# Folding an output gate into the output weights, and moving a bias product one chunk earlier, in a DiT attention block

## The chip, the cores and the metric

The kernel runs on one core of one Trainium2 chip. The metric is the device time of one execution in microseconds (us). The engines are called PE (matmul), Vector or DVE, Scalar or ACT, GpSimd or POOL, and SP, whose queue issues the loads and stores. The kernel's tiles lie in SBUF, but for those that PE writes its results to, which lie in PSUM. A run counts as slow when it is over 1.5% above the fastest run of the same kernel, otherwise as fast. Medians are of all runs of a kernel, ratios of its fast runs alone.

## The reference, cut to what matters

```python
B, N, D = 2, 256, 1152          # all bf16
mod = (silu(c) @ w_mod).reshape(B, 6, 1, D)
shift_a, scale_a, gate_a = mod[:, 0], mod[:, 1], mod[:, 2]
h = layernorm(x) * (1 + scale_a) + shift_a
q, k, v = split(h @ wqkv)
p = softmax(q @ k.T * D ** -0.5)
out = x + gate_a * ((p @ v) @ wo)
```

`gate_a` has one value per batch and output column. Multiplying the result by it is therefore the same as multiplying the columns of `wo` by it, once per batch.

## The kernel before: the parts that matter

There are four row tiles of 128 tokens, two per batch, and nine chunks of 128 along D. k is computed from the scaled rows alone, `hTk`, because a shift of k changes all scores of a row by the same amount, which the softmax removes. q and v need `hT = hTk + shift`. The shift comes out of 81 small matmuls (`m_shift`), which stand between the k chunks. In program order, the last 36 of them follow the last k chunk:

```python
k_chunks([0, 1])                     # per chunk: 9 matmuls 128x128 by 128x512, one cast to SBUF
for j in range(2, KC):
    k_chunks([j])
    if j == 6: m_shift.do(range(0, 5))
    if j == 8:
        m_shift.do(range(5, KC))
        make_hT()                    # copies shiftT out of PSUM, then 18 adds of 128x256,
                                     # dealt out to Vector, GpSimd, Scalar in turn
q_chunks([0, 1])
for j in range(2, KC): q_chunks([j])
```

The gate is computed and broadcast over the partitions between the v tiles (81 small matmuls, then 18 broadcasts by matmul, cast to `gate_bc`). The output stage applies it with two Vector operations per tile:

```python
for tt in range(TT):
    for (f0, fw) in FB:              # (0, 512), (512, 512), (1024, 128)
        ... ps = sum over dk of oT[:, dk, tt] x wo_sb[:, dk, f0:f0+fw] ...
        nc.vector.scalar_tensor_tensor(out=tmp, in0=ps, scalar=rinv[:, tt:tt+1],
                                       in1=gate_bc[:, b, f0:f0+fw], op0=mult, op1=mult)
        nc.vector.tensor_tensor(out=y, in0=tmp, in1=x_sb[:, tt, f0:f0+fw], op=add)
        nc.sync.dma_start(out=out_flat[...], in_=y)
```

PE's results for q, k, v and y rotate through three PSUM tiles (pool `ps_acc`). Vector and Scalar share the casts that empty the q, k and v ones; Vector empties those of y.

## Time and profile before

| | before |
|---|---|
| time, median of the first 4 runs | 107.05 us (106.48 to 108.79) |
| span in the profile | 104.7 us |
| PE busy | 97.3 us, 93% |
| Vector busy | 43.9 us, 42% |

The page's first part gives each engine's busy time, share of the span and instruction count. Its second cuts the span into 40 slices of 2.6 us; a digit is the busy share in tenths. PEld is the loading of weights for PE, PEclk the share of its clock that PE was granted.

```profile
PE 97.3 (93%) x786; PEld 54.0 (52%) x786; DVE 43.9 (42%) x100; ACT 25.2 (24%) x60; POOL 6.3 (6%) x14
...
PE   5996998999999699999999999999999999999940
...
DVE  1696229302202342220221552232257847678780
...
PEclk9999999999999999999999999999999999999999
```

PE is full from the eighth slice on, except for one dip (the 6 in slice 14, about 36 us) and the end. Vector is idle more than half of the time. So only three things can shorten this kernel with the same matmuls: the first 16 us, the dip, and the tail.

The dip in the timeline of the kernel before. Columns: start and length in us, engine, source line, operation, outputs and inputs, count; in brackets the idle time of the engine before it and who ended it.

```profile
34.62 1.04 PE L75 MATMUL ps_shift<-scT,wm_sh 128*128 128x2 bf16 x36
...
35.70 0.18 DVE L313 COPY shiftT<-ps_shift 128x18 f32<-128x18 f32 x1 [2.13 <-PE ps_shift L75]
35.91 1.77 DVE L322 TENSOR_SCALAR hT<-hTk,shiftT 128x256 bf16<-128x256 bf16 x6
35.98 2.50 ACT L327 ACTIVATE hT<-hTk,shiftT 128x256 bf16<-128x256 bf16 x6 [0.57 <-DVE shiftT L313]
...
36.60 1.67 PE L75 MATMUL ps_q<-hT,wq_sb 128*128 128x512 bf16 x7 [0.93 <-POOL hT L324]
```

The shift products end, the shift is copied out, the first two pieces of `hT` are made, and only then can q start: PE is idle 0.93 us.

The tail in the timeline of the kernel before:

```profile
82.97 17.71 PE L75 MATMUL ps_y<-wo_sb,oT 128*128 128x512 bf16 x108
...
99.06 0.69 DVE L462 TENSOR_TENSOR y<-tmp,x_sb 128x512 bf16<-128x512 f32 x1
100.22 1.01 DVE L457 SCALAR_TENSOR_TENSOR tmp<-ps_y,rinv,gate_bc 128x512 f32<-128x512 f32 x2 [0.47 <-PE ps_y L75]
101.14 0.89 DVE L462 TENSOR_TENSOR y<-tmp,x_sb 128x512 bf16<-128x512 f32 x2
```

After the last matmul Vector still runs one pass over the last two tiles (512 and 128 wide), then a second one. Before that, Vector waited for PE at the y tiles, as the waits view says (who waited for whom; total us, times, longest):

```profile
DVE tmp L457 <- PE ps_y L75: 5.3, 8, 1.5
...
PE ps_q L75 <- POOL hT L324: 0.9, 1, 0.9
```

No line of that view has PE waiting for Vector in the y stage. The two operations per y tile cost time only at the very end.

### The profile page before, as it was taken

The numbers are of one execution on the slowest core, as the hardware profiler recorded it, in microseconds if no ns is written. First come the engines' busy times: TensorE is split into PE (matmuls) and PEld (weight loads), VectorE is DVE, ScalarE is ACT, GpSimd is POOL, SyncE is SP. The second block draws the span as 40 slices with busy tenths as digits, with TensorE's granted clock in tenths as the row PEclk, the third lists the DMA queues.
The fourth block names the chain that finished last, engine by engine and source line by source line (L and its number), as shares of the span: only waits on it lengthen the run. The fifth ranks groups of instructions, "written<-read, shape, count | busy, mean of one in ns | idle before, by whom it ended". The sixth has DMA issues, their size and how long they took to land.

```text
span 104.7 us, 1898 instructions
## 1 busy us (share of the span) xinstructions
PE 97.3 (93%) x786; PEld 54.0 (52%) x786; DVE 43.9 (42%) x100; ACT 25.2 (24%) x60; POOL 6.3 (6%) x14
## 2 busy tenths in 40 slices
PE   5996998999999699999999999999999999999940
PEld 2325774444464544444447846664599745555420
DVE  1696229302202342220221552232257847678780
ACT  4079017220120472022022541110246500000000
POOL 2044000000000280000000000000000000000000
PEclk9999999999999999999999999999999999999999
DMA  2999957999999999999999900000000001222212
GB/s 68 351 370 367 387 132 193 312 329 384 392 370 330 326 332 356 387 390 390 394 391 358 254 12 6 0 0 0 6 0 3 0 0 50 69 87 76 65 51 63
DMA packets 19332, 21.07 MB, mean 201 GB/s; under 512 B 2811, under 2 KB 14203, under 8 KB 19323
## 3 DMA queue, kind: packets, MB, share of 16 engines
q1 hardware_dynamic: 19323, 20.95, 60.6%
q8 instruction: 6, 0.10, 0.4%
q14 instruction: 3, 0.02, 0.1%
HBM read 19.76 MB, written 1.18 MB: 200 GB/s over the span
## 4 chain that ended last, share of the span: by engine, by line
PE 61%; issue 26%; DVE 6%; DMA 3%; POOL 1%; POOLq 1%; DVEq 0%
PE ps_q L75 17%; PE ps_v L75 17%; PE ps_y L75 16%; PE ps_o L75 4%; PE ps_s L75 4%; DVE stats L171 3%; DMA x_sb<-in_x_dram 3%; PE ps_gate L75 2%; POOL xn L225 1%; PE ps_g L75 1%; DVE tmp L457 1%; DVE y L462 1%; POOLq L489 1%; DVE mv L175 0%; PE ps_p L78 0%
## 5 line engine op out<-in xcount | busy, mean ns | idle before, releaser
L75 PE MATMUL ps_v<-wv_sb,hT 128*128 128x512 bf16 (+1 forms) x108 | 19.2, 325 | 0.0
L75 PE MATMUL ps_q<-hT,wq_sb 128*128 128x512 bf16 x81 | 17.6, 379 | 0.9 <-POOL hT L324 0.9
L75 PE MATMUL ps_k<-hTk,wk_sb 128*128 128x512 bf16 x81 | 17.8, 379 | 0.3 <-DVE hTk L296 0.3
L75 PE MATMUL ps_y<-wo_sb,oT 128*128 128x512 bf16 (+1 forms) x108 | 17.7, 326 | 0.0
L75 PEld LDWEIGHTS <-oT 128*128 128x128 bf16 x108 | 9.2, 98 | 8.5
L75 PEld LDWEIGHTS <-wq_sb 128*128 128x128 bf16 x81 | 7.9, 98 | 10.2 <-issue 0.9
L75 PEld LDWEIGHTS <-wk_sb 128*128 128x128 bf16 x81 | 7.7, 98 | 9.9 <-issue 0.8
L75 PEld LDWEIGHTS <-hT 128*128 128x128 bf16 x108 | 8.9, 98 | 7.1
L457 DVE SCALAR_TENSOR_TENSOR tmp<-ps_y,rinv,gate_bc 128x512 f32<-128x512 f32 (+1 forms) x12 | 7.0, 615 | 5.3 <-PE ps_y L75 5.3
L141 DVE CAST qT<-ps_q 128x512 bf16<-128x512 f32 x5 | 3.5, 692 | 13.8 <-PE ps_q L75 13.8
L141 DVE CAST kT<-ps_k 128x512 bf16<-128x512 f32 x4 | 2.8, 692 | 12.3 <-PE ps_k L75 12.3
L141 DVE CAST v_sb<-ps_v 128x512 bf16<-128x512 f32 x5 | 3.5, 691 | 7.7 <-PE ps_v L75 7.2
L139 ACT CAST kT<-ps_k 128x512 bf16<-128x512 f32 x5 | 2.9, 586 | 14.9 <-PE ps_k L75 14.9
L462 DVE TENSOR_TENSOR y<-tmp,x_sb 128x512 bf16<-128x512 f32 (+1 forms) x12 | 6.3, 553 | 0.1
L75 PE MATMUL ps_w<-zeros 128*128 128x512 bf16 x10 | 4.4, 632 | 1.2 <-DVE zeros L124 1.2
L171 DVE BATCH_NORM_STATS2 stats<-x_sb 128x6 f32<-128x384 bf16 x9 | 4.5, 537 | 2.4 <-DMA x_sb<-in_x_dram 2.4
L139 ACT CAST v_sb<-ps_v 128x128 bf16<-128x128 f32 (+1 forms) x7 | 2.8, 403 | 10.5 <-PE ps_v L75 10.3
L139 ACT CAST qT<-ps_q 128x512 bf16<-128x512 f32 x4 | 2.3, 586 | 12.1 <-PE ps_q L75 12.1
L141 DVE CAST gate_bc<-ps_g 128x512 bf16<-128x512 f32 (+1 forms) x6 | 3.2, 555 | 3.4 <-PE ps_g L75 3.3
L324 POOL TENSOR_SCALAR hT<-hTk,shiftT 128x256 bf16<-128x256 bf16 x6 | 3.0, 515 | 26.0 <-DVE shiftT L313 26.0
L75 PEld LDWEIGHTS <-wm_sc 128*128 128x128 bf16 x94 | 3.3, 96 | 2.0 <-issue 1.3
L75 PE MATMUL ps_s<-kT,qT 128*128 128x256 bf16 x36 | 4.1, 272 | 0.0
(62 smaller groups left out, 78.5 us busy)
## 6 DMA issues: line engine op xcount, KB each, us to landing
wm_sc<-in_w_mod_dram SPq DMA_DIRECT2D x9, 288.0 KB, 5.3
wm_sh<-in_w_mod_dram SPq DMA_DIRECT2D x9, 288.0 KB, 6.4
wq_sb<-in_wqkv_dram SPq DMA_DIRECT2D x3, 864.0 KB, 10.5
wm_g<-in_w_mod_dram SPq DMA_DIRECT2D x9, 288.0 KB, 7.4
wo_sb<-in_wo_dram SPq DMA_DIRECT2D x9, 288.0 KB, 6.0
wv_sb<-in_wqkv_dram SPq DMA_DIRECT2D x2, 1152.0 KB, 9.7
x_sb<-in_x_dram SPq DMA_DIRECT2D x4, 288.0 KB, 3.5
wk_sb<-in_wqkv_dram SPq DMA_DIRECT2D x2, 576.0 KB, 5.5
```

Of the source, the lines that this page charges most:

```text
L75: return _pin(nc.tensor.matmul(*a, **kw))
L139: nc.scalar.copy(out=out_ap, in_=in_ap)
L141: nc.vector.tensor_copy(out=out_ap, in_=in_ap)
L171: pin("dve", nc.vector.bn_stats(out=stats_t[tt][:, s, :], in_=x_sb[:, tt, s * SUBW:(s + 1) * SUBW]))
L225: nc.gpsimd.tensor_scalar(out=xn[:, tt, :], in0=x_sb[:, tt, :], scalar1=rstd[:, 0:1], scalar2=nmr[:, 0:1], op0=ALU.mult, op1=ALU.add,)
L324: nc.gpsimd.tensor_scalar(out=o_ap, in0=i_ap, scalar1=1.0, scalar2=shiftT[:, k, b:b + 1], op0=ALU.mult, op1=ALU.add)
L457: nc.vector.scalar_tensor_tensor(out=tmp[:, :fw], in0=ps[:, :fw], scalar=rinv[:, tt:tt + 1], in1=gate_bc[:, b, f0:f0 + fw], op0=ALU.mult, ...
L462: nc.vector.tensor_tensor(out=y[:, :fw], in0=tmp[:, :fw], in1=x_sb[:, tt, f0:f0 + fw], op=ALU.add)
L489: with _tile.TileContext(nc) as tc:
```

## The change

The intent: scale `wo` by the gate beforehand, once per batch (the fold: 18 multiplications of 128x1152, nine per batch), while Vector has time, so that the epilogue is one operation; compute the gate early enough for that; and make `hT` behind the last k chunk instead of after it.

```diff
-    load_cols(wv_sb, Wv, 0, 512)
     wm_g = wmpool.tile(...); load_rows(wm_g, w_mod[:, 2 * D:3 * D], range(KC))
+    load_cols(wv_sb, Wv, 0, 512)
...
-                # hT adds on Vector, GpSimd and Scalar in turn
+                nc.vector.tensor_scalar_add(hT[...], hTk[...], shiftT[:, k, b:b + 1])
...
-        if j == 6:
+        if j == 5:
             m_shift.do(range(0, 5))
-        if j == 8:
+        if j == 7:
             m_shift.do(range(5, KC))
             make_hT()
... # m_gate.do and gate_bcast move from between the v tiles to between the q chunks
+    wo_g = [wpool.tile([P, KC, D], BF16, name="wo_g0", tag="wk"),    # in the place of wk and wq
+            wpool.tile([P, KC, D], BF16, name="wo_g1", tag="wq")]
+    def fold_gate(b, dk, eng):
+        e = nc.vector if eng == "dve" else nc.gpsimd
+        e.tensor_tensor(out=wo_g[b][:, dk, :], in0=wo_sb[:, dk, :], in1=gate_bc[:, b, :], op=ALU.mult)
... # 9 folds after p_transposes(1, 0), 9 after v_tile(1, 2), all on Vector
-                mm(..., rhs=wo_sb[:, dk, f0:f0 + fw], ...)
-            tmp = ps * rinv * gate_bc        # scalar_tensor_tensor
-            y = tmp + x_sb                   # tensor_tensor
+                mm(..., rhs=wo_g[b][:, dk, f0:f0 + fw], ...)
+            y = ps * rinv + x_sb             # scalar_tensor_tensor
```

The rest of the diff renames helpers. The compiler's scheduler spreads the 18 folds among the score maxima and the casts of v in Vector's order.

More of the change, by code (lines that the diff above doesn't have):

```diff
@@ L56 @@
     _nosync = mybir.DependencyInfo(mybir.DependencyClass.NoSync, mybir.DependencyReason.DATA)
-    _pe_prev = [None]
-    def _pin(inst):
-        if _pe_prev[0] is not None:
-            tc.add_manual_dep(inst.ins, _pe_prev[0].ins.name, _nosync, reason="pe order")
-        _pe_prev[0] = inst
-        return inst
     _chains = {}
@@ L74, in mm @@
     def mm(*a, **kw):
-        return _pin(nc.tensor.matmul(*a, **kw))
+        return pin("pe", nc.tensor.matmul(*a, **kw))
     def tr(*a, **kw):
-        return _pin(nc.tensor.transpose(*a, **kw))
+        return pin("pe", nc.tensor.transpose(*a, **kw))
     x_sb = act.tile([P, TT, D], BF16, name="x_sb")
@@ L97 @@
     wm_sh = wmpool.tile([P, KC, D], BF16, name="wm_sh", tag="wm")
-    wk_sb = wpool.tile([P, KC, D], BF16, name="wk_sb")
-    wq_sb = wpool.tile([P, KC, D], BF16, name="wq_sb")
+    wk_sb = wpool.tile([P, KC, D], BF16, name="wk_sb", tag="wk")
+    wq_sb = wpool.tile([P, KC, D], BF16, name="wq_sb", tag="wq")
     wv_sb = wpool.tile([P, KC, D], BF16, name="wv_sb")
@@ L153, in do @@
                 for j in range(KC):
-                    mm(
-                        self.ps[:, j, :], lhsT=self.wm[:, k, j * P:(j + 1) * P], rhs=scT[:, k, :],
-                        start=self.first, stop=(k == KC - 1 and j == KC - 1), skip_group_check=True,
-                    )
+                    mm(self.ps[:, j, :], lhsT=self.wm[:, k, j * P:(j + 1) * P], rhs=scT[:, k, :],
+                       start=self.first, stop=(k == KC - 1 and j == KC - 1), skip_group_check=True)
                     self.first = False
@@ L162 @@
     SUBW = D // NSUB
+    stats_t = {}
     mvs = {}
-    stats_t = {}
     def ln_bnstats(tt, subs):
@@ L175, in ln_aggr, with ln_rstd, ln_act_mean @@
         pin("dve", nc.vector.bn_aggr(out=mv[:], in_=stats_t[tt][:]))
-        mvs[tt] = (mv, None, None)
-    def ln_rstd(tt):
-        mv = mvs[tt][0]
+        mvs[tt] = [mv[:, 0:1], mv[:, 1:2], None, None]
+    def ln_rstd(tt, var_scale=1.0):
         lnv = small.tile([P, 1], FP32, name="lnv")
-        pin("act", nc.scalar.activation(out=lnv[:], in_=mv[:, 1:2], func=ACT.Ln, bias=eps_t[:, 0:1], scale=1.0))
+        pin("act", nc.scalar.activation(out=lnv[:], in_=mvs[tt][1], func=ACT.Ln, bias=eps_t[:, 0:1],
+                                        scale=var_scale))
         rstd = small.tile([P, 1], FP32, name="rstd")
         pin("act", nc.scalar.activation(out=rstd[:], in_=lnv[:], func=ACT.Exp, scale=-0.5))
-        mvs[tt] = (mv, rstd, None)
+        mvs[tt][2] = rstd[:, 0:1]
     def ln_nmr(tt):
-        mv, rstd, _ = mvs[tt]
         nmr = small.tile([P, 1], FP32, name="nmr")
-        pin("dve", nc.vector.scalar_tensor_tensor(out=nmr[:], in0=mv[:, 0:1], scalar=-1.0, in1=rstd[:],
+        pin("dve", nc.vector.scalar_tensor_tensor(out=nmr[:], in0=mvs[tt][0], scalar=-1.0, in1=mvs[tt][2],
                                                   op0=ALU.mult, op1=ALU.mult))
-        mvs[tt] = (mv, rstd, nmr)
-    def ln_stats_UNUSED(tt, need_nmr):
-        mv = None
-        rstd = None
-        mvs[tt] = (mv, rstd, None)
-    def ln_stats_act_mean(tt):
+        mvs[tt][3] = nmr[:, 0:1]
+    def ln_act_mean(tt):
         mean = small.tile([P, 1], FP32, name="mean_a")
@@ L203, in ln_stats_act_mean, with ln_act_var @@
         pin("act", nc.scalar.activation(out=negmean[:], in_=mean[:], func=ACT.Copy, scale=-1.0))
-        mvs[tt] = (mean, negmean)
-    def ln_stats_act_var(tt):
-        mean, negmean = mvs[tt]
+        mvs[tt] = [mean[:, 0:1], None, None, negmean[:, 0:1]]
+    def ln_act_var(tt):
         ssq = small.tile([P, 1], FP32, name="ssq_a")
-        pin("act", nc.scalar.activation(out=xn[:, tt, :], in_=x_sb[:, tt, :], func=ACT.Square, bias=negmean[:, 0:1],
-                                        scale=1.0, accum_out=ssq[:, 0:1]))
-        lnv = small.tile([P, 1], FP32, name="lnv")
-        pin("act", nc.scalar.activation(out=lnv[:], in_=ssq[:], func=ACT.Ln, bias=eps_t[:, 0:1], scale=1.0 / D))
-        rstd = small.tile([P, 1], FP32, name="rstd")
-        pin("act", nc.scalar.activation(out=rstd[:], in_=lnv[:], func=ACT.Exp, scale=-0.5))
-        mvs[tt] = (mean, rstd, None)
+        pin("act", nc.scalar.activation(out=xn[:, tt, :], in_=x_sb[:, tt, :], func=ACT.Square,
+                                        bias=mvs[tt][3], scale=1.0, accum_out=ssq[:, 0:1]))
+        mvs[tt][1] = ssq[:, 0:1]
+        ln_rstd(tt, var_scale=1.0 / D)
     def ln_norm(tt, eng):
-        mv, rstd, nmr = mvs[tt]
+        mean, _, rstd, nmr = mvs[tt]
         if eng == "dve":
-            pin("dve", nc.vector.tensor_scalar(
-                out=xn[:, tt, :], in0=x_sb[:, tt, :], scalar1=mv[:, 0:1], scalar2=rstd[:, 0:1],
-                op0=ALU.subtract, op1=ALU.mult,
-            ))
-        else:
-            nc.gpsimd.tensor_scalar(
-                out=xn[:, tt, :], in0=x_sb[:, tt, :], scalar1=rstd[:, 0:1], scalar2=nmr[:, 0:1],
-                op0=ALU.mult, op1=ALU.add,
-            )
+            pin("dve", nc.vector.tensor_scalar(out=xn[:, tt, :], in0=x_sb[:, tt, :], scalar1=mean, scalar2=rstd,
+                                               op0=ALU.subtract, op1=ALU.mult))
+        else:
+            nc.gpsimd.tensor_scalar(out=xn[:, tt, :], in0=x_sb[:, tt, :], scalar1=rstd, scalar2=nmr,
+                                    op0=ALU.mult, op1=ALU.add)
     ptiles = [ps_tr.tile([P, 2, TT, P], BF16, name=f"ps_xT{g}", tag="tr") for g in range(4)]
@@ L242 @@
     ln_rstd(0)
-    ln_stats_act_mean(3)
+    ln_act_mean(3)
     ln_bnstats(1, range(2)); ln_nmr(0); ln_bnstats(1, [2]); ln_aggr(1)
@@ L251 @@
     ln_rstd(1)
-    ln_stats_act_var(3)
+    ln_act_var(3)
     ln_bnstats(2, range(2))
@@ L255 @@
     pin("dve", nc.vector.reciprocal(out=e_t[:], in_=e_t[:]))
-    pin("dve", nc.vector.tensor_tensor(
-        out=scT[:].rearrange("p k b -> p b k"),
-        in0=ps_c[:].rearrange("p (b k) -> p b k", b=B),
-        in1=e_t[:].rearrange("p (b k) -> p b k", b=B),
-        op=ALU.mult,
-    ))
+    pin("dve", nc.vector.tensor_tensor(out=scT[:].rearrange("p k b -> p b k"),
+                                       in0=ps_c[:].rearrange("p (b k) -> p b k", b=B),
+                                       in1=e_t[:].rearrange("p (b k) -> p b k", b=B), op=ALU.mult))
     ln_nmr(1); ln_bnstats(2, [2]); ln_aggr(2)
@@ L287 @@
     ACT_CHUNKS = (1, 4, 6)
-    mcnt = 0
     for k in range(KC):
@@ L301, with proj_chunks @@
     shiftT = const.tile([P, KC, B], FP32, name="shiftT")
-    def k_chunks(js):
-        pss = [ps_acc.tile([P, T], FP32, name="ps_k", tag="acc") for _ in js]
+    def proj_chunks(w_sb, src, dst, js, nm):
+        pss = [ps_acc.tile([P, T], FP32, name=nm, tag="acc") for _ in js]
         for k in range(KC):
             for ji, j in enumerate(js):
-                mm(pss[ji][:], lhsT=wk_sb[:, k, j * P:(j + 1) * P], rhs=hTk[:, k, :],
-                                 start=(k == 0), stop=(k == KC - 1))
+                mm(pss[ji][:], lhsT=w_sb[:, k, j * P:(j + 1) * P], rhs=src[:, k, :],
+                   start=(k == 0), stop=(k == KC - 1))
         for ji, j in enumerate(js):
-            evac(kT[:, j, :], pss[ji][:])
+            evac(dst[:, j, :], pss[ji][:])
     def make_hT():
         nc.vector.tensor_copy(out=shiftT[:], in_=m_shift.ps[:])
-        engs = ["dve", "pool", "act"]
-        cnt = 0
         for k in range(KC):
             for b in range(B):
-                o_ap = hT[:, k, b * N:(b + 1) * N]
-                i_ap = hTk[:, k, b * N:(b + 1) * N]
-                e = engs[cnt % 3]
-                if e == "dve":
-                    nc.vector.tensor_scalar_add(o_ap, i_ap, shiftT[:, k, b:b + 1])
-                elif e == "pool":
-                    nc.gpsimd.tensor_scalar(out=o_ap, in0=i_ap, scalar1=1.0,
-                                            scalar2=shiftT[:, k, b:b + 1], op0=ALU.mult, op1=ALU.add)
-                else:
-                    nc.scalar.activation(out=o_ap, in_=i_ap, func=ACT.Identity,
-                                         scale=1.0, bias=shiftT[:, k, b:b + 1])
-                cnt += 1
-    k_chunks([0, 1])
+                nc.vector.tensor_scalar_add(hT[:, k, b * N:(b + 1) * N], hTk[:, k, b * N:(b + 1) * N],
+                                            shiftT[:, k, b:b + 1])
+    proj_chunks(wk_sb, hTk, kT, [0, 1], "ps_k")
     for j in range(2, KC):
-        k_chunks([j])
-        if j == 6:
+        proj_chunks(wk_sb, hTk, kT, [j], "ps_k")
+        if j == 5:
             m_shift.do(range(0, 5))
-        if j == 8:
+        if j == 7:
             m_shift.do(range(5, KC))
@@ L340, with gate_bcast @@
     qT = act.tile([P, KC, T], BF16, name="qT", tag="C")
-    def q_chunks(js):
-        pss = [ps_acc.tile([P, T], FP32, name="ps_q", tag="acc") for _ in js]
-        for k in range(KC):
-            for ji, j in enumerate(js):
-                mm(pss[ji][:], lhsT=wq_sb[:, k, j * P:(j + 1) * P], rhs=hT[:, k, :],
-                   start=(k == 0), stop=(k == KC - 1))
-        for ji, j in enumerate(js):
-            evac(qT[:, j, :], pss[ji][:])
-    q_chunks([0, 1])
-    for j in range(2, KC):
-        q_chunks([j])
+    gateT = const.tile([P, KC, B], BF16, name="gateT")
+    gate_bc = act.tile([P, B, D], BF16, name="gate_bc")
+    m_gate = ModT(wm_g, "gate")
+    def gate_bcast(b, j0):
+        jn = min(4, KC - j0)
+        ps_g = ps_tr.tile([P, T], FP32, name="ps_g", tag="tr")
+        for jj in range(jn):
+            j = j0 + jj
+            mm(ps_g[:, jj * P:(jj + 1) * P], lhsT=gateT[:, j, b:b + 1].to_broadcast([P, P]),
+               rhs=ident[:], start=True, stop=True)
+        evac(gate_bc[:, b, j0 * P:(j0 + jn) * P], ps_g[:, :jn * P])
+    proj_chunks(wq_sb, hT, qT, [0, 1], "ps_q")
+    for j in range(2, KC):
+        proj_chunks(wq_sb, hT, qT, [j], "ps_q")
+        if j == 4:
+            m_gate.do(range(0, 3))
+        if j == 5:
+            m_gate.do(range(3, 6))
+        if j == 6:
+            m_gate.do(range(6, 9))
+            nc.vector.tensor_copy(out=gateT[:], in_=m_gate.ps[:])
+        if j == 7:
+            gate_bcast(0, 0)
+            gate_bcast(0, 4)
+        if j == 8:
+            gate_bcast(0, 8)
+            gate_bcast(1, 0)
+    wo_g = [wpool.tile([P, KC, D], BF16, name="wo_g0", tag="wk"),
[3 more added lines that the diff above has]
+        e.tensor_tensor(out=wo_g[b][:, dk, :], in0=wo_sb[:, dk, :], in1=gate_bc[:, b, :], op=ALU.mult)
     FB = [(0, 512), (512, 512), (1024, 128)]
@@ L360 @@
     pT = act.tile([P, B, QT, N], BF16, name="pT")
-    gateT = const.tile([P, KC, B], BF16, name="gateT")
-    gate_bc = act.tile([P, B, D], BF16, name="gate_bc")
-    m_gate = ModT(wm_g, "gate")
     def v_tile(fi, tt):
@@ L368, in v_tile @@
         for k in range(KC):
-            mm(ps[:, :fw], lhsT=hT[:, k, tt * P:(tt + 1) * P],
-                             rhs=wv_sb[:, k, f0:f0 + fw],
-                             start=(k == 0), stop=(k == KC - 1))
+            mm(ps[:, :fw], lhsT=hT[:, k, tt * P:(tt + 1) * P], rhs=wv_sb[:, k, f0:f0 + fw],
+               start=(k == 0), stop=(k == KC - 1))
         evac(v_sb[:, tt, f0:f0 + fw], ps[:, :fw])
@@ L377, in scores @@
         for dk in range(KC):
-            mm(ps_s[:, :N], lhsT=qT[:, dk, tq * P:(tq + 1) * P],
-                             rhs=kT[:, dk, b * N:(b + 1) * N],
-                             start=(dk == 0), stop=(dk == KC - 1))
+            mm(ps_s[:, :N], lhsT=qT[:, dk, tq * P:(tq + 1) * P], rhs=kT[:, dk, b * N:(b + 1) * N],
+               start=(dk == 0), stop=(dk == KC - 1))
         mx = small.tile([P, 1], FP32, name="mx")
@@ L393, in p_transposes @@
         evac(pT[:, b, :, qi * P:(qi + 1) * P], ps_p[:, 0, :QT, :])
-    def gate_bcast(b, j0):
-        jn = min(4, KC - j0)
-        ps_g = ps_tr.tile([P, T], FP32, name="ps_g", tag="tr")
-        for jj in range(jn):
-            j = j0 + jj
-            mm(ps_g[:, jj * P:(jj + 1) * P], lhsT=gateT[:, j, b:b + 1].to_broadcast([P, P]),
-                             rhs=ident[:], start=True, stop=True)
-        evac(gate_bc[:, b, j0 * P:(j0 + jn) * P], ps_g[:, :jn * P])
     v_tile(0, 0)
+    gate_bcast(1, 4)
+    gate_bcast(1, 8)
     scores(0, 0)
@@ L413 @@
     p_transposes(0, 1)
-    m_gate.do(range(0, 3))
     v_tile(0, 3)
     p_transposes(1, 0)
-    m_gate.do(range(3, 6))
+    for dk in range(KC):
+        fold_gate(0, dk, "dve")
     v_tile(1, 0)
     p_transposes(1, 1)
-    m_gate.do(range(6, 9))
-    nc.vector.tensor_copy(out=gateT[:], in_=m_gate.ps[:])
     v_tile(1, 1)
     v_tile(1, 2)
-    gate_bcast(0, 0)
+    for dk in range(KC):
+        fold_gate(1, dk, "dve")
     v_tile(1, 3)
-    gate_bcast(0, 4)
     v_tile(2, 0)
-    gate_bcast(0, 8)
     v_tile(2, 1)
-    gate_bcast(1, 0)
     v_tile(2, 2)
-    gate_bcast(1, 4)
     v_tile(2, 3)
-    gate_bcast(1, 8)
     oT = act.tile([P, KC, T], BF16, name="oT", tag="B")
@@ L444 @@
                     mm(ps_o[:, dd * N:(dd + 1) * N], lhsT=v_sb[:, b * QT + kt, dk * P:(dk + 1) * P],
-                                     rhs=pT[:, b, kt, :], start=(kt == 0), stop=(kt == QT - 1))
+                       rhs=pT[:, b, kt, :], start=(kt == 0), stop=(kt == QT - 1))
             evac(oT[:, dk0:dk0 + dn, b * N:(b + 1) * N], ps_o[:, :dn * N].rearrange("p (a n) -> p a n", a=dn))
@@ L452 @@
             for dk in range(KC):
-                mm(ps[:, :fw], lhsT=oT[:, dk, tt * P:(tt + 1) * P],
-                                 rhs=wo_sb[:, dk, f0:f0 + fw],
-                                 start=(dk == 0), stop=(dk == KC - 1))
-            tmp = work.tile([P, 512], FP32, name="tmp")
-            nc.vector.scalar_tensor_tensor(
-                out=tmp[:, :fw], in0=ps[:, :fw], scalar=rinv[:, tt:tt + 1],
-                in1=gate_bc[:, b, f0:f0 + fw], op0=ALU.mult, op1=ALU.mult,
-            )
+                mm(ps[:, :fw], lhsT=oT[:, dk, tt * P:(tt + 1) * P], rhs=wo_g[b][:, dk, f0:f0 + fw],
+                   start=(dk == 0), stop=(dk == KC - 1))
             y = work.tile([P, 512], BF16, name="y")
-            nc.vector.tensor_tensor(out=y[:, :fw], in0=tmp[:, :fw], in1=x_sb[:, tt, f0:f0 + fw], op=ALU.add)
+            nc.vector.scalar_tensor_tensor(out=y[:, :fw], in0=ps[:, :fw], scalar=rinv[:, tt:tt + 1],
+                                           in1=x_sb[:, tt, f0:f0 + fw], op0=ALU.mult, op1=ALU.add)
             nc.sync.dma_start(out=out_flat[tt * P:(tt + 1) * P, f0:f0 + fw], in_=y[:, :fw])
```

## The prediction

> **What bounds it now.** The tensor engine. In the page's busy table PE is busy 97.3 of 104.7 us (93%); by stretch it is busy 100% from 36.6 to 100.2 us (q, v, scores, output), at full clock. Vector is busy 42%. The matmuls stay 786, so only PE's gaps and the two ends can be gained.
>
> The gaps the change can touch:
> 1. Before q. The waits view shows PE idle 0.93 us before the first ps_q, ended by the GpSimd hT add: the shift product ends at 35.66, then come the shiftT copy and hT adds, and ps_q starts at 36.60. The 81 ps_q then take 17.64 us where the v-tile pace (1.94 us per 9) gives 17.44: 0.2 us lost to hT pieces.
> 2. The tail. The last 128x512 ps_y is done at 100.2. Then tmp 512 (751 ns), tmp 128 (343), y 512 (687), y 128 (286); the last store is issued at 102.28 and lands at 103.8.
>
> **What the change does.**
> - Shift products are one k chunk earlier, so shiftT and hT overlap chunk 8 (1.94 us). hT goes to Vector alone: 18 adds. In the trace Vector's hT add beside GpSimd takes 364 ns (295 from start to start); I estimate 0.21-0.28 us alone, which keeps up with q's 0.43 us per two pieces. The first wq third landed at 34.92, before q would start at 35.66. Saving 0.9-1.1 us.
> - tmp+y become one op, PSUM input, about 0.75 us as tmp. At the tail the last store goes out at about 101.4: saving 0.85 us. Other y tiles gain nothing: Vector waited for PE.
> - Gate products and broadcasts move from v into q. Same PE work: zero. wm_g is loaded before the first wv part, so it lands about 3 us earlier (by 47), wanted from 45.4 to 50: in time.
> - New: 18 folds wo*gate, 128x1152 bf16 on Vector, scheduled between the score maxima and the v casts. [...] No op of this kind is in the trace.
>
> **Where folds could cost.** The ps_v tiles rotate over three buffers, PE makes one in about 2.05 us. On the scheduled order Vector does two folds and one 692 ns cast per ps_v: 2.1-2.2 us. I reckon the first Vector v cast about 2.5-3 us late, later ones 3.3-4 us late, where about 3.4 is free. So PE stalls 0 to 0.6 us in v; I take 0.25. Folds end near 77, before y starts (82).
>
> **Sum.** -1.0 (q start) -0.85 (tail) +0.25 = -1.6 us of 107.05: 105.4 us, range 104.6 to 106.5. Chances: faster by over 2% 0.25, within 2% 0.69, slower 0.06.
>
> **What would show it.** (a) the wait ps_q <- hT is gone and ps_q directly follows ps_k; (b) one Vector op after the last ps_y, last store issued about 0.85 us sooner after the last ps_y than before; (c) fold mean 0.70-0.80 us; (d) PE waits on v casts under 0.6 us in total; (e) no wait of ps_y for wo_g, and no wait for wm_g or wv.
>
> **What would make it wrong.** [...] 24 us of Vector work would stall v by 4 us or more, making it slower. hT adds alone as slow as 0.36 us from start to start: q stalls over 1 us in its first pair. A late wm_g or wo row would hold PE or Vector. No stall at all and hT perfect: -2 us, close to the 2% line.

The sum came to -1.6 us: -1.0 for the start of q, -0.85 for the tail, +0.25 for stalls of PE in v. The trace after has 750 ns for a fold, by which two folds and a cast of 692 ns add up to 2.19 us. What 24 us of folds do is measured in e8 (18 times 1345 ns). The 0.21-0.28 us of an hT add was an estimate; the trace before has 273 to 509 ns, with GpSimd and Scalar adding as well.

## The result

| | before | after |
|---|---|---|
| median | 106.98 us (16 runs, 106.48 to 108.79) | 104.98 us (11 runs, 104.50 to 105.66) |
| span in the profile | 104.7 us | 102.9 us |

The ratio is 0.9823, with a 95% interval of 0.9799 to 0.9847. The gain of 1.8% is clear of noise, and lies across the 2% line with its interval.

The page of the kernel after, the same parts:

```profile
PE 97.0 (94%) x786; PEld 53.8 (52%) x786; DVE 50.6 (49%) x118; ACT 22.4 (22%) x54; POOL 3.3 (3%) x8
...
PE   5996998999999999999999999999999999999970
...
DVE  1596309312011962220224999999924844233450
```

The dip is gone. Vector has more work than before, a solid row of nines from slice 23 to 29, and lower digits in the last ten slices.

Timeline of the kernel after, at the start of q:

```profile
32.86 1.04 PE L67 MATMUL ps_shift<-scT,wm_sh 128*128 128x2 bf16 x36
...
33.77 2.10 PE L67 MATMUL ps_k<-hTk,wk_sb 128*128 128x512 bf16 x9
33.94 0.18 DVE L284 COPY shiftT<-ps_shift 128x18 f32<-128x18 f32 x1 [0.19 <-PE ps_shift L67]
34.15 3.03 DVE L287 TENSOR_SCALAR hT<-hTk,shiftT 128x256 bf16<-128x256 bf16 x15
...
35.70 1.67 PE L67 MATMUL ps_q<-hT,wq_sb 128*128 128x512 bf16 x7
```

The copy and the adds run while PE does the last k chunk; `ps_q` starts with no bracket, that is with no idle time before it. The tail, and one stretch of the v stage, in the timeline of the kernel after:

```profile
67.32 0.68 DVE L133 CAST v_sb<-ps_v 128x512 bf16<-128x512 f32 x1
67.92 1.42 DVE L335 TENSOR_TENSOR wo_g<-wo_sb,gate_bc 128x1152 bf16<-128x1152 bf16 x2
...
68.14 0.28 PE L70 MATMUL ps_p<-ident,p_all 128*128 128x128 bf16 x2
...
69.25 0.68 DVE L133 CAST v_sb<-ps_v 128x512 bf16<-128x512 f32 x1
...
82.08 17.71 PE L67 MATMUL ps_y<-wo_g,oT 128*128 128x512 bf16 x108
...
99.33 1.01 DVE L420 SCALAR_TENSOR_TENSOR y<-ps_y,rinv,x_sb 128x512 bf16<-128x512 f32 x2 [1.19 <-PE ps_y L67]
```

At the tail one Vector pass is left. In the v stage Vector alternates between a cast and two folds. The v tile that ended when `ps_p` began (68.14, its last results about 0.2 us later) was cast from 69.25 on, about 0.9 us late.

The time from the first instruction to the first `ps_k` differs from run to run (16.0 to 18.6 us among the profiles with the same head), with the arrival of the first loads and, in the slowest of them (e9's), a lower clock there: its mean over the span is 0.984, with 1.00 in every window from 16 to 94 us and `ps_y` at its usual pace up to 103.5 us. Spans of single profiles are therefore poor to compare. The stretches between the first starts of PE's groups repeat to 0.02 us in kernels with the same code in them, and the table is worked out from those starts:

| stretch, us | before | after | difference |
|---|---|---|---|
| first ps_k to first ps_q | 20.58 | 19.51 | -1.07 |
| first ps_q to first ps_v | 17.48 | 20.24 | +2.76 |
| first ps_v to first ps_o | 24.96 | 22.21 | -2.75 |
| first ps_o to first ps_y | 3.93 | 3.93 | 0.00 |
| first to last ps_y | 17.49 | 17.49 | 0.00 |
| last ps_y to the end | 4.21 | 3.36 | -0.85 |

The gate's matmuls moved from v to q and cost the same there (2.76 against 2.75 us). What is left is 1.07 us at the start of q and 0.85 us at the tail, 1.92 us in all, beside 2.0 us between the medians.

### The profile page after: what moved, and what is told of

It reads as the page before. It is cut to its first block, busy times and chain, and to the rows that moved or that the text cites. A ratio compares the mean times of both kernels' runs of the same rounds, so it can differ in the third digit from the quotient of the medians.

```text
span 102.9 us, 1906 instructions
## 1 busy us (share of the span) xinstructions
PE 97.0 (94%) x786; PEld 53.8 (52%) x786; DVE 50.6 (49%) x118; ACT 22.4 (22%) x54; POOL 3.3 (3%) x8
## 4 chain that ended last, share of the span: by engine, by line
PE 81%; DMA 12%; SPq 2%; issue 1%; DVEq 0%; DVE 0%
PE ps_k L67 17%; PE ps_v L67 17%; PE ps_q L67 17%; PE ps_y L67 17%; DMA wm_sc<-in_w_mod_dram 6%; DMA x_sb<-in_x_dram 4%; PE ps_o L67 4%; PE ps_s L67 4%; DMA wk_sb<-in_wqkv_dram 2%; PE ps_shift L67 2%; PE ps_gate L67 2%; SPq L74 1%; PE ps_g L67 1%; SPq L80 1%; DVEq L448 0%
## 5 line engine op out<-in xcount | busy, mean ns | idle before, releaser
L67 PE MATMUL ps_v<-wv_sb,hT 128*128 128x512 bf16 (+1 forms) x108 | 18.3, 326 | 0.0
L67 PE MATMUL ps_q<-hT,wq_sb 128*128 128x512 bf16 x81 | 18.3, 379 | 0.0
L67 PE MATMUL ps_y<-wo_g,oT 128*128 128x512 bf16 (+1 forms) x108 | 17.7, 326 | 0.0
L335 DVE TENSOR_TENSOR wo_g<-wo_sb,gate_bc 128x1152 bf16<-128x1152 bf16 x18 | 13.0, 750 | 0.0
L420 DVE SCALAR_TENSOR_TENSOR y<-ps_y,rinv,x_sb 128x512 bf16<-128x512 f32 (+1 forms) x12 | 7.0, 614 | 10.6 <-PE ps_y L67 10.6
L133 DVE CAST v_sb<-ps_v 128x512 bf16<-128x512 f32 (+1 forms) x8 | 4.7, 586 | 2.9 <-PE ps_v L67 2.9
L67 PE MATMUL ps_scale<-scT,wm_sc 128*128 128x2 bf16 x81 | 3.3, 163 | 1.0 <-DVE nmr L177 1.0
L67 PE MATMUL ps_o<-pT,v_sb 128*128 128x256 bf16 x36 | 4.1, 273 | 0.0
L67 PE MATMUL ps_w<-wm_sc 128*128 128x512 bf16 x13 | 4.1, 376 | 0.0
```

The lines of the kernel that those rows point to most:

```text
L67: return pin("pe", nc.tensor.matmul(*a, **kw))
L133: nc.vector.tensor_copy(out=out_ap, in_=in_ap)
L335: e.tensor_tensor(out=wo_g[b][:, dk, :], in0=wo_sb[:, dk, :], in1=gate_bc[:, b, :], op=ALU.mult)
L420: nc.vector.scalar_tensor_tensor(out=y[:, :fw], in0=ps[:, :fw], scalar=rinv[:, tt:tt + 1], in1=x_sb[:, tt, f0:f0 + fw], op0=ALU.mult, op1= ...
```

## The experiments

Theory A: the gain is the sum of two independent parts. The head start of one k chunk takes away the gap before q, and the short epilogue pays at the last tile alone. Rivals: that freeing Vector from GpSimd closes the gap (B); that the shorter epilogue pays all along the output stage (C). A further question is why the folds cost nothing, where I had expected up to 0.6 us. All runs gave correct results.

| run | ratio to before | 95% interval | ps_k to ps_q | ps_v to ps_y | last ps_y to end |
|---|---|---|---|---|---|
| before | | | 20.58 | 28.89 | 4.21 |
| after | 0.9823 | 0.9799 to 0.9847 | 19.51 | 26.14 | 3.36 |
| e1_shift_and_dve | 0.9899 | 0.9872 to 0.9927 | 19.51 | 28.89 | 4.22 |
| e2_shift_only | 0.9894 | 0.9870 to 0.9918 | 19.60 | 28.89 | 4.21 |
| e3_dve_only | 0.9992 | 0.9964 to 1.0020 | 20.52 | 28.89 | 4.21 |
| e4_fold_only | 0.9935 | 0.9909 to 0.9962 | 20.60 | 26.35 | 3.37 |
| e5_no_fold | 0.9918 | 0.9854 to 0.9982 | 19.51 | 26.14 | 4.21 |
| e6_fold_b1 | 0.9833 | 0.9786 to 0.9880 | 19.51 | 26.14 | 3.36 |
| e7_three_more | 0.9823 | 0.9788 to 0.9857 | 19.50 | 26.14 | 3.36 |
| e9_nine_more | 0.9958 | 0.9899 to 1.0016 | 19.51 | 27.68 | 3.36 |
| e8_fold_fp32 | 1.0537 | 1.0464 to 1.0611 | 19.50 | 34.14 | 3.36 |

The last three columns are us between first starts, as above; from ps_v to ps_y, kernels with the gate in q have 2.75 us less than those with it in v. In e4 the records of two ps_y matmuls are missing, probably the first among them, so its 26.35 is too long by one matmul (the stretch behind it is shorter by the same 0.22).

### The two parts of the change alone

e1_shift_and_dve, from the kernel before:

```diff
-        if j == 6:
+        if j == 5:
             m_shift.do(range(0, 5))
-        if j == 8:
+        if j == 7:
             m_shift.do(range(5, KC))
             make_hT()
...
-        engs = ["dve", "pool", "act"]
+        engs = ["dve", "dve", "dve"]
```

> The kernel before with two edits: shift products one k chunk earlier, and the hT adds all on Vector. No gate move, no fold, old two-op epilogue. Theory A (the change is worth the sum of two independent parts, this one and the tail): the 0.93 us idle before ps_q goes to 0, ps_q takes 17.4 to 17.5 us, the tail is as before; 1.0 to 1.1 us less, ratio about 0.990. Rival (the parts only pay together, or the fold pays all): within 0.3 us of the kernel before.

It gave 1.0% and removed the same 1.07 us before q as the whole change, with the long tail intact. e2_shift_only has the edits of j alone:

> Only the shift products one chunk earlier; hT still on Vector, GpSimd and Scalar in turn. Theory A (the head start of one chunk, 1.94 us, is what counts): the idle before ps_q is 0 here too, 0.9 to 1.1 us less, ratio about 0.990. Rival B (freeing Vector from GpSimd is what counts): the idle before ps_q stays above 0.5 us, ratio above 0.995.

It gave the same within noise; 0.09 us of the 1.07 is lost again. Its timeline at the start of q:

```profile
33.99 0.18 DVE L313 COPY shiftT<-ps_shift 128x18 f32<-128x18 f32 x1 [0.19 <-PE ps_shift L75]
...
34.27 3.00 POOL L324 TENSOR_SCALAR hT<-hTk,shiftT 128x256 bf16<-128x256 bf16 x6 [24.11 <-DVE shiftT L313]
35.79 5.57 PE L75 MATMUL ps_q<-hT,wq_sb 128*128 128x512 bf16 x25
```

GpSimd still adds, for 3.0 us, and PE does not wait. e3_dve_only has the edit of the engines alone:

> Only hT on Vector alone; the shift products stay behind the last k chunk. Theory A: the copy of shiftT and the first two adds (0.18, 0.28, 0.28 us, starting 0.21 us apart) still lie between ps_shift and ps_q, so the idle before ps_q is 0.7 to 0.8 us instead of 0.93 and ps_q takes 17.4 to 17.6 us; 0.2 to 0.4 us less, ratio 0.996 to 0.998. Rival B: the idle goes to near 0, ratio about 0.990.

```profile
36.52 0.18 DVE L313 COPY shiftT<-ps_shift 128x18 f32<-128x18 f32 x1 [2.13 <-PE ps_shift L75]
36.73 3.61 DVE L322 TENSOR_SCALAR hT<-hTk,shiftT 128x256 bf16<-128x256 bf16 x18
37.36 3.83 PE L75 MATMUL ps_q<-hT,wq_sb 128*128 128x512 bf16 x16 [0.88 <-DVE hT L322]
```

The idle time is 0.88 us instead of 0.93, and the time did not change. I had expected 0.7 to 0.8: what lies between is a chain of copy, adds and hand-over, and I had left out the hand-over. The first matmul of q reads two adds. They ended 0.69 us after the start of the copy instead of 0.84, but `ps_q` then started 0.15 us after them instead of 0.05 (the end of an add on GpSimd is rough in these profiles). Rival B falls; it was the head start.

The adds themselves did become faster. The tile view gives least, median and greatest duration in ns. In the kernel before:

```profile
L322 DVE TENSOR_SCALAR hT<-hTk,shiftT x6: 273/354/509, 35.9 to 37.3; 128x256 bf16<-128x256 bf16 x6
```

and in the kernel after:

```profile
L287 DVE TENSOR_SCALAR hT<-hTk,shiftT x18: 275/277/286, 34.2 to 37.5; 128x256 bf16<-128x256 bf16 x18
```

With GpSimd and Scalar adding as well, the six adds on Vector took 273 to 509 ns in the kernel before and 275 to 506 ns in e2; with all 18 on Vector they took 275 to 286 ns in the kernel after, 277 to 286 in e1 and 277 to 285 in e3. No run here shows what lengthens some of them beside the other engines.

### The fold alone, and half of it

e4_fold_only is the changed kernel with the shift products back at j == 6 and j == 8 and the three-engine adds.

> The changed kernel with the shift products and the three-engine hT put back as before; the gate move, fold and one-op epilogue stay. Theory A: the idle of about 0.9 us before ps_q is back, the tail is the short one (last store issued about 0.85 us sooner after the last ps_y), no PE wait in v or y; 0.85 to 0.95 us less than before, ratio about 0.992. Rival (one op less per y tile pays all along the output stage): PE would have waited for Vector in ps_y before, which its trace does not show, and the gain would be well over 1 us.

The gap before q is back, as its waits view says, the tail is short, and the ratio is 0.9935. The two parts alone, 1.0% and 0.65%, add up to 1.7%, beside 1.8% for both.

```profile
PE ps_q L67 <- POOL hT L295: 0.9, 1, 0.9
```

In e5_no_fold the changed kernel loses the folds and has the old pair of operations again, with the gate still in q.

> The changed kernel without the fold: gate products and broadcasts stay in q, wo stays unscaled, the epilogue is the old pair of Vector ops. Theory A (the gate move itself is worth nothing): same as the run with the shift products and hT alone, ratio about 0.990; tail long again (about 4.5 us from the last 128x512 ps_y to the end instead of 3.6). Rival (moving the gate out of v helps by itself): clearly below 0.987.

It lands at e1, as theory A says: 0.9918, with a wide interval, and the stretches of e1 but for the moved gate: from first ps_q to first ps_y both take 46.37 us. Moving the gate is worth nothing by itself. In e6_fold_b1 only the second batch is folded:

```diff
-    for dk in range(KC):
-        fold_gate(0, dk, "dve")
...
+            if b == 0: (the old pair of operations, with wo_sb)
+            else:      (the one operation, with wo_g[1])
```

> The changed kernel with half of the fold: only batch 1 (the last two row tiles) gets the scaled copy of wo and the one-op epilogue; batch 0 keeps wo and the pair of ops. Theory A (only the last tile's epilogue is on the critical path): same as the changed kernel, ratio about 0.982, with 9 folds, 6.7 us, of Vector work fewer. Rival C (each shorter epilogue pays): half of the fold's gain is lost, ratio about 0.986.

The ratio of 0.9833 has too wide an interval to tell 0.982 from 0.986. The waits view does tell:

```profile
DVE y L426 <- PE ps_y L67: 4.5, 4, 1.4
...
DVE tmp L418 <- PE ps_y L67: 3.1, 4, 1.5
```

Vector waits for PE in both batches, with one operation per tile and with two; the stretches are those of the changed kernel to 0.01 us. Half of the folds bought nothing. Rival C falls.

### Why the folds cost nothing, and when they would

e7_three_more does three of the folds twice, e9_nine_more nine of them:

```diff
-        e.tensor_tensor(out=wo_g[b][:, dk, :], ...)
+        for _ in range(2 if b == 0 and dk < 3 else 1):      # e9: 2 if b == 1 else 1
+            e.tensor_tensor(out=wo_g[b][:, dk, :], ...)
```

> The changed kernel with 3 of the 18 folds done twice, 2.0 us more Vector work in v, at starts 0.67 us apart. The scheduler puts 3 of the folds between the last but one and the last v cast of 512. As predicted (casts 3 to 4 us late, the slack used up): PE stalls 2 us or more in v, ratio about 1.00. By the trace after (casts at most 1.0 us late, Vector idle 1.9 us before that last cast): no PE stall, ratio about 0.982.

The time stayed at 0.9823 and no stretch changed. From e7's timeline:

```profile
74.14 2.76 DVE L336 TENSOR_TENSOR wo_g<-wo_sb,gate_bc 128x1152 bf16<-128x1152 bf16 x4
76.81 0.69 DVE L133 CAST v_sb<-ps_v 128x512 bf16<-128x512 f32 x1
```

Four folds in a row fit into the time in which Vector had been idle. My picture, in which the slack was used up, is refuted. Then nine more:

> The changed kernel with the 9 folds of batch 1 done twice, 6.0 us more Vector work; the last 512-wide v cast then stands behind 26 folds in Vector's order. From the starts of the trace after (0.67 us from fold to fold, 5.0 us of other work from 57.1 on) that cast ends at about 80 us instead of 77, while the v tile that needs its PSUM buffer is wanted at 77.3: PE stalls about 3 to 4 us in v, ratio about 1.015. If Vector work in v is free as long as the engine has idle time in total (49% busy after), no stall and ratio 0.982.

```profile
76.09 6.10 DVE L336 TENSOR_TENSOR wo_g<-wo_sb,gate_bc 128x1152 bf16<-128x1152 bf16 x9
82.11 0.69 DVE L133 CAST v_sb<-ps_v 128x512 bf16<-128x512 f32 x1
...
83.77 2.84 DVE L133 CAST oT<-ps_o 128x512 bf16<-128x512 f32 x5
```

PE's side of it, the same kernel:

```profile
80.54 0.66 PE L67 MATMUL ps_v<-wv_sb,hT 128*128 128x128 bf16 x9 [0.35 <-ACT v_sb L131]
...
83.72 2.43 PE L67 MATMUL ps_o<-pT,v_sb 128*128 128x256 bf16 x19 [0.66 <-DVE v_sb L133]
```

Now PE does stall: 1.54 us more from first ps_v to first ps_y (this profile is slow, with a mean clock of 0.984, but the clock was 1.00 in every window from 16 to 94 us, and so in this stretch; the two fast runs, 106.5 and 106.6 us, are 1.5 to 1.6 us above the changed kernel's median). I had expected 3 to 4 us, because I let the late cast block a PSUM buffer that the third v tile after it would need. In the trace all v tiles are done by 81.2, before that cast begins at 82.11, so none of them waited for it. The last of them did wait for a cast of Scalar (0.35 us idle), and the first `ps_o` came 0.52 us later than in the changed kernel. The larger part of the cost, 1.02 us, came a step later, where `ps_o` of the second batch reads the late `v_sb`. So idle time in total is not the measure (Vector is 49% busy in the changed kernel): what counts is which cast stands behind which folds, and when PE reads it.

e8_fold_fp32 keeps the broadcast gate in fp32:

```diff
-    gate_bc = act.tile([P, B, D], BF16, name="gate_bc")
+    gate_bc = act.tile([P, B, D], FP32, name="gate_bc")
```

> The changed kernel with the broadcast gate kept in fp32, so that the fold has one 4-byte operand; all else the same. [...] about 1.35 us each, 24 us in all; the last 512-wide v cast ends near 85 us, and the part of ps_o that needs it waits for it: PE loses 5 to 7 us before y, ratio about 1.04. [...]

What was tested: whether a fold with a 4-byte operand takes longer, about 1.35 us, or stays at 0.75 us, with the ratio at 0.982.

The tile view of e8:

```profile
L335 DVE TENSOR_TENSOR wo_g<-wo_sb,gate_bc x18: 1342/1345/1348, 57.9 to 84.6; 128x1152 bf16<-128x1152 bf16 x18
```

The fold takes 1345 ns instead of 750, and the kernel is 5% slower than before the change. (The view's label still writes bf16 for the operands; only the gate's type was changed.) The trace before has adds of the same kind: those of y (L462), also `tensor_tensor`, have one operand in fp32 (tmp) and one in bf16 (x_sb), and took 286 ns at 128 columns and 687 ns at 512. An estimate from these two, 1.04 ns per further column, is 1355 ns for 1152; the 1345 ns here are within 1% of it. PE lost more than the time in which it waited. Its timeline in e8, and the clock by stretch (the columns are length, then busy time of PE, PEld, DVE, ACT and POOL with counts, then the granted share of the clock):

```profile
79.46 2.02 PE L67 MATMUL ps_o<-pT,v_sb 128*128 128x256 bf16 x17
86.85 4.23 PE L67 MATMUL ps_o<-pT,v_sb 128*128 128x256 bf16 x19 [5.37 <-DVE v_sb L133]
```

```profile
79.00:82.00 3.00, 2.48 (x26) 2.03 (x25) 3.00 (x3) 1.17 (x2) 0.00 (x0) 1.00 0.00 0
82.00:85.00 3.00, 0.00 (x0) 0.00 (x0) 3.00 (x4) 0.00 (x0) 0.00 (x0) 0.89 0.00 0
...
87.00:88.00 1.00, 1.00 (x6) 0.70 (x5) 1.00 (x2) 0.37 (x1) 0.00 (x0) 0.50 0.00 0
...
91.00:92.00 1.00, 1.00 (x6) 0.41 (x5) 0.42 (x1) 0.27 (x1) 0.00 (x0) 0.91 0.00 0
```

The clock was 1.00 from 79 to 82, fell in the 5.4 us in which PE was idle, and was 0.50 from 85 until about 91: 19 matmuls of `ps_o` lasted 4.0 us up to the first `ps_y`, where they last 2.1 us at full clock (19 times 0.109 us, the pace of the 36 in 3.93 us). From first ps_v to first ps_y the trace has 8.0 us more than the changed kernel, where I had expected 5 to 7; about 2.0 us of them are the half clock (4.0 us less 2.1), and the 6.1 us left are inside that range. The clock fell about 2.9 us after the last matmul ended, at 81.5 (an estimate: 0.89 as the mean of 82 to 85 means 0.50 from about 84.3 on, if the clock went from 1.00 to 0.50 in one step). Whether the idle time made it fall, and how much of it that takes, no run here shows. This profile, 113.66 us, counts as slow, just over 1.5% above the fastest run. Two of the four runs, 111.95 and 113.50 us, count as fast, though their mean clocks were 0.980 and 0.968, so the 5% include time at a lower clock too.

### Attempts to beat the changed kernel

PE has no gap left between 16 and 99.8 us, so the head and the tail remain. x1_tail cuts the last row tile differently and issues the very last store from Scalar's queue:

```diff
-        for (f0, fw) in FB:
+        for (f0, fw) in (FB if tt < TT - 1 else [(0, 512), (512, 448), (960, 192)]):
...
-            nc.sync.dma_start(out=out_flat[...], in_=y[:, :fw])
+            q = nc.scalar if (tt == TT - 1 and f0 + fw == D) else nc.sync
+            q.dma_start(out=out_flat[...], in_=y[:, :fw])
```

> An attempt to beat the changed kernel at the tail only: the last row tile is cut 512, 448, 192 instead of 512, 512, 128, so that the last but one epilogue is done by the time the last ps_y is, and the very last store is issued by Scalar's queue instead of behind the other one. From the changed kernel's tail (last store issued at 100.5, 0.16 us after the last Vector op) about 0.2 us less: ratio about 0.980, hard to tell from 0.982 by time; the profile's distance from the last ps_y to the end should be 0.1 to 0.3 us shorter.

Median 104.87 us (104.55 to 104.94), ratio 0.9798 (0.9770 to 0.9827). From the last ps_y to the end the trace has 3.18 us instead of 3.36. It is the fastest kernel of this study by its trace, by 0.18 us; by device time it can't be told from the changed one. The two edits were made at once; what each is worth stays open.

x2_head drops the ten warming matmuls (`warm` in the kernel) between the scale products and loads wk in whole rows; x3_both adds the tail of x1:

```diff
-    WBLK = [2, 2, 1, 2, 1, 1, 0, 1, 3]
+    WBLK = [0] * 8 + [3]
-    (wk in pieces of 256 columns, per row block, then by columns)
+    load_rows(wk_sb, Wk, range(KC))
-    proj_chunks(wk_sb, hTk, kT, [0, 1], "ps_k")
+    proj_chunks(wk_sb, hTk, kT, [0, 1, 2], "ps_k")
```

> An attempt at the head only: the 10 warming matmuls (0.21 us each) between the scale products are dropped (the 3 behind the last stay), wk is loaded in whole rows instead of 512-byte pieces, and three k chunks run together over the first rows. In the trace after, the last scale product stands at 14.83 though its rows landed by about 13.5, and PE is busy from 8.9 on. If the warming matmuls delay it: ps_k starts about 1 us sooner, and with the rows landing every 0.75 us the first three chunks are done 0.5 to 1.1 us sooner; ratio 0.972 to 0.977. Rival: without them the matmuls fall to half rate, or the whole rows land too late: ratio 0.982 or above.

> Both attempts together: the sum of the two, ratio about 0.970 to 0.975 if both hold.

Both failed: 105.66 us, ratio 0.9874 (0.9838 to 0.9910), and 105.04 us, ratio 0.9826 (0.9789 to 0.9863). In x2's profile `ps_k` did start sooner (15.38), but the rows then arrived no faster than PE used them (its weight loads waited 2.8 us for wk in all), and ps_k to ps_q took 20.67 us instead of 19.51: 0.8 us won at the start, 1.2 us lost behind it. In three of six runs of each the mean granted clock was 0.965 to 0.983, where the changed kernel had 0.995 or more in all twelve. x3's profile is one of those, and the page shows where (the row of the granted clock):

```profile
PEclk9999557999999999999999999999999999999999
```

The clock is at half in slices 5 and 6 and part of 7, from about 10 us on, where the warming matmuls had been: nine `ps_xT` matmuls that take 0.66 us in x2's profile take 1.12 us there. That the warming matmuls prevent this is not shown: x2's profile lacks them too and has 0.9 or more in all these slices, e9's has them and yet a mean clock of 0.984, with 1.00 in every window from 16 to 94 us, and two edits were made at once. Nor is the clock the whole of it. x2's full-clock runs took 105.27 to 105.84 us, and its quickest run, 105.11 us, had 0.983. Which edit costs how much in the full-clock runs (104.75 to 105.03 in x3) stays open.

## Why the prediction was right, point by point

The prediction was 105.4 us (104.6 to 106.5); measured were 104.98 us.

- **The start of q, "-1.0".** Right: -1.07 us between starts. (The idle time of 0.93 us counts from the modelled end of the matmul before, so it is a little less than the delay.) e2 shows that the head start does it.
- **"0.2 us lost to hT pieces" inside q.** Wrong, though it did not spoil the sum. From the first to the last `ps_q` start the trace before has 17.26 us, and e1 17.27. The 17.64 us of the timeline runs to the modelled end of the last matmul, 379 ns, while matmuls start 216 ns apart. I had compared a stretch that includes that end with a pace that doesn't.
- **The tail, "-0.85".** Right: 4.21 to 3.36 us.
- **hT adds, "0.21-0.28 us alone".** Right: 277 ns each, 0.20 us from start to start.
- **Folds, "fold mean 0.70-0.80 us".** Right: 750 ns. Neither wm_g nor wv held PE or Vector: the last row of wm_g landed at 46.9 us, as foretold ("by 47").
- **Stall, "PE stalls 0 to 0.6 us in v; I take 0.25".** This term was mis-sized: 0.00 us. I put the casts of v 2.5 to 4 us late; they were 0.5 to 1.1 us late. From cast to cast, with two folds between, Vector took 1.94 us where I had 2.1 to 2.2, so it gained on PE (2.05 us per v tile) instead of falling behind. I had added up durations (two folds of 750 ns and a cast of 692 ns are 2.19 us) where Vector's instructions overlap: two folds in a row take 1.42 us, so the second starts 0.67 us after the first, and the same 0.06 to 0.09 us is saved at most other places in the row. Over the 18 instructions from the first fold to the first of these casts that is about 1.5 us; the rest of my error there was a rough sum by hand that I can't assign to one term. e9 shows the same over nine folds in a row: 6.10 us, 0.67 us from start to start. Also, three buffers in turn were too strict a model, as e9 showed. That I predicted a small term all the same was partly luck: it was the difference between two figures of 3 to 4 us, the delay and the slack, and the delay was too large by 2 to 3 us.
- **The sum.** -1.07 - 0.85 + 0 = -1.92 us, where I had -1.6; nearly all of the difference is the stall that did not come.

## What to carry to other kernels

Read an epilogue's worth from the last tile alone when the engine that runs it waits for PE at all the others: half of the fold gave all of its gain. A small product that others wait for belongs one block of work ahead of its reader; the position was worth 0.98 us alone (e2), the choice of engine 0.06 alone (e3) and 0.09 once the position is moved (e1 against e2). Add up an engine's work by start-to-start times (0.67 us per fold here), not by durations (0.75 us), and judge extra work by which reader stands behind it.
